# Loading the first quarter of W1 ahead of everything else, and writing the order of the start by hand

## The chip, the core and the metric

The kernel runs on one core of a Trainium2 chip. The metric is the device time of one launch in microseconds. The core's engines work beside each other, each through its own list of instructions in order: TensorE (matrix products), VectorE, ScalarE, GpSimd, and SyncE, which here only issues transfers (DMAs).

## What is computed

Eight batches of 576 rows and 512 columns go through an attention with 32 memory slots per head, a normalised MLP and a gated MLP:

```
a = softmax(phi, over the sequence);  k_m, v_m = a^T k, a^T v      # 8 heads, 32 slots, 64 columns
x = softmax(q k_m^T / 8) v_m                                       # heads side by side: 512 columns
x = x + relu(layernorm(x) * g_ln @ w_ch1) @ w_ch2                  # 512 -> 2048 -> 512
u, v = halves of gelu(x @ w_in)
out = x + (u * (w_sg @ (layernorm(v) * g2) + b_sg)) @ w_out
```

The weights `w_ch1` (W1) and `w_ch2` (W2) come as 64-bit floats, 8.4 MB each.

## The kernel before

`phase1` computes the attention and the first MLP, `phase2` the rest. The first MLP never forms the attention's output for its first product: per batch it multiplies the slot values with the scaled and column-centred W1 (`make_vw`, tiles VW, evicted by `evict_vw` as a high and a low half), and the product `m1` (L592) takes the attention weights aT, high and low, times VW. `relu` splits the result for `m2` (L622 to L624), which multiplies it with the split W2. W1 is used in four quarters of 512 columns, W2 in 16 chunks of 128 rows. For batch 0 the order is: quarter 0 for the first block (256 rows, two tiles of 128) and the second block (320 rows, two tiles of 128 and one of 64), then quarter 1 for both, and so on. `m2` follows three steps behind `m1`.

Ahead of the first `m1` stand the steps of batch 0. `load_phi`, `load_kv`, `load_rem` and `load_q` issue transfers, all through `load` (L85) on SyncE. `prep_max` reduces phi over the sequence on VectorE, transposes on TensorE and lays the maxima on a diagonal (dg); `prep_exp` spreads them, subtracts and takes Exp; `prep_sum` adds on GpSimd and transposes the sums (ptsum); `prep_kv` makes the kv products; `prep_norm` scales them (kvn); `prep_T` transposes (ptk, kvT). `t_q` transposes q, `t_scores` multiplies and starts the softmax on the tile z, `t_norm` and `t_attn` finish it, and `t_attn` writes aT: the high half on ScalarE, the low half on GpSimd for the first two tiles and on VectorE for the others. For W1, `load_w1` brings a quarter in as four raw tiles of 512 KB (two transfers each), `scale_w1` converts them from 64 to 32 bits (`to_f32`: Prelu on ScalarE L112, shift and merge on VectorE L113 and L114) and scales them (ScalarE L498); `center_w1` forms the column means on TensorE (cm, L504) and subtracts them on VectorE (L506, two halves); `store_w1` writes the quarter back for later batches. `split_w2` converts a chunk of W2 with the same steps and splits it.

Every step has a planned time (`at_time`), in units of 1/18 of a batch, and the program is written in the order of these times; negative times lie before the first `m1`. A scheduler that runs when the kernel is built then reorders the instructions of each engine by its own estimate, within their dependencies and within the orders stated by `issue_after`. In the kernel before, gains, phi, k, v and q come first, and the first W1 quarter is loaded at -26.5, scaled at -16.5, the second quarter scaled at -5.0 and centred at -0.3.

## Time and profile before

| | us |
|---|---|
| median of 3 runs | 1208.59 |
| lowest and highest run | 1206.55, 1211.44 |
| span of the profiled execution | 1206.0 |
| first `m1` of batch 0 in it | 49.82 |
| TensorE busy in it | 1167.4 (97%) |

The profile shows one execution. PE is TensorE, PEld its loading of weights, DVE VectorE, ACT ScalarE, POOL GpSimd, SP SyncE; L592 is a line of the kernel. A timeline row has start, duration, engine, line, operation, what it writes and reads, and in brackets the idle time before it with what ended it. In the table of stages each engine has its busy time and, in brackets, its count; the clock is the share of TensorE's full clock that was granted, and a DMA share of 1 is 16 engines full. A busy TensorE counts the whole time of overlapping products, so it is not TensorE at its peak.

### The profile page before, as it was taken

Reading aid. Unit: us, or ns where it says so; the run is one execution under the profiler, and the core shown is the slowest. Engines: PE = TensorE matmul, PEld = TensorE weight load, DVE = VectorE, ACT = ScalarE, POOL = GpSimd, SP = SyncE. Lnnn points to the kernel's source line nnn. Section 1 sums busy time; section 2 is a strip of 40 time slices with the busy share of each in tenths; the row PEclk is TensorE's granted clock in tenths of the full one; section 3 lists DMA queues with packets and bytes.
Section 4 is the critical chain, followed back from the end, with each engine's and each line's share of the span. In section 5 each row is a group of like instructions: output and inputs, shape, how many; then the busy total and the mean of one; then the engine's idle time right before and its main releaser. Section 6 shows DMA issues by size and latency. Waiting matters only on the chain.

```text
span 1206.0 us, 20725 instructions
## 1 busy us (share of the span) xinstructions
PE 1167.4 (97%) x7711; PEld 991.3 (82%) x7711; DVE 689.7 (57%) x1669; ACT 467.1 (39%) x1071; POOL 400.7 (33%) x622
## 2 busy tenths in 40 slices
PE   4699999999999999999999999999999999999998
PEld 2377678888788888788888888889989988998997
DVE  2887665755645545644645445568576477447532
ACT  3575333332432322332323445445444354344430
POOL 2133212211201211201211112456666475566641
PEclk9699999999999999999999999999999999999999
DMA  8996744373341443331410343122240042022201
GB/s 205 284 287 177 219 106 125 79 205 66 109 117 31 129 137 66 97 107 23 128 36 27 106 118 115 35 82 88 77 143 18 19 142 77 1 81 86 79 18 70
DMA packets 199141, 124.15 MB, mean 103 GB/s; under 512 B 93312, under 2 KB 174336, under 8 KB 199040
## 3 DMA queue, kind: packets, MB, share of 16 engines
q1 hardware_dynamic: 199040, 122.82, 36.4%
q8 instruction: 61, 1.00, 0.3%
q14 instruction: 40, 0.33, 0.1%
HBM read 99.72 MB, written 31.33 MB: 109 GB/s over the span
## 4 chain that ended last, share of the span: by engine, by line
PE 86%; DVE 5%; DMA 4%; SPq 2%; issue 1%; POOL 1%; ACT 1%; POOLq 0%; DVEq 0%
PE ph L592 16%; PE py L622 10%; PE py L624 10%; PE py L623 10%; PE pvs L1027 8%; PE po L1050 8%; PE pv L918 8%; PE pu L1002 7%; PE pvw L544 2%; DMA raw<-in_moe_w_ch_dram 2%; SPq L85 2%; PE kvp L315 1%; DMA q<-q_d 1%; PE cm L504 1%; PE sc L401 1%
## 5 line engine op out<-in xcount | busy, mean ns | idle before, releaser
L592 PE MATMUL ph<-aTh,vw 128*128 128x320 f32 (+1 forms) x1024 | 247.2, 300 | 3.5 <-ACT aTh L440 1.4
L622 PE MATMUL py<-whl,hh 128*128 128x512 f32 x512 | 201.8, 396 | 3.0 <-ACT hh L578 3.0
L592 PEld LDWEIGHTS ph<-aTh,vw 128*128 128x128 f32 x1024 | 178.2, 190 | 28.3 <-issue 9.4
L623 PE MATMUL py<-whl,hh 128*128 128x512 f32 x512 | 201.3, 393 | 0.0
L624 PE MATMUL py<-whl,hl 128*128 128x512 f32 x512 | 183.2, 397 | 0.0
L578 ACT ACTIVATE hh<-ph 128x256 fp32r<-128x256 f32 x256 | 96.6, 385 | 167.7 <-PE ph L592 111.5
L579 DVE SCALAR_TENSOR_TENSOR hl<-ph,hh 128x256 fp32r<-128x256 f32 x256 | 106.5, 421 | 87.6 <-ACT hh L578 87.0
L592 PE MATMUL ph<-aTl,vw 128*128 128x256 f32 (+1 forms) x512 | 152.2, 297 | 0.0
L1027 PE MATMUL pvs<-wsh,vhl 128*128 128x288 f32 x576 | 121.0, 295 | 0.0
L622 PEld LDWEIGHTS py<-whl,hh 128*128 128x128 f32 x512 | 96.3, 188 | 26.9 <-ACT hh L578 5.7
L623 PEld LDWEIGHTS py<-whl,hh 128*128 128x128 f32 x512 | 96.5, 189 | 19.3 <-issue 0.8
L1002 PE MATMUL pu<-yTh,whl 128*128 128x288 f32 x512 | 111.0, 296 | 0.3 <-DVE ug L907 0.3
L592 PEld LDWEIGHTS ph<-aTl,vw 128*128 128x128 f32 x512 | 97.1, 190 | 10.3 <-issue 2.9
L624 PEld LDWEIGHTS py<-whl,hl 128*128 128x128 f32 x512 | 89.9, 189 | 12.0 <-issue 2.3
L1027 PEld LDWEIGHTS pvs<-wsh,vhl 128*128 128x128 f32 x576 | 94.4, 188 | 0.6
L918 PE MATMUL pv<-whl,yTh 128*128 128x512 f32 x288 | 91.0, 396 | 0.0
L1050 PE MATMUL po<-whl,gh 128*128 128x512 f32 x288 | 90.0, 391 | 0.0
L1002 PEld LDWEIGHTS pu<-yTh,whl 128*128 128x128 f32 x512 | 85.4, 189 | 1.8 <-DVE ug L907 0.8
L578 ACT ACTIVATE cr<-ph 128x64 fp32r<-128x64 f32 x128 | 28.6, 226 | 130.7 <-PE ph L592 130.1
L1030 POOL TENSOR_TENSOR gt<-gt,ug 128x288 f32<-128x288 f32 x64 | 52.8, 826 | 68.5 <-DVE gt L1029 62.1
L1027 PE MATMUL pvs<-wsl,vhl 128*128 128x288 f32 x256 | 75.6, 295 | 0.0
L1002 PE MATMUL pu<-yTl,whl 128*128 128x288 f32 x256 | 75.5, 295 | 0.0
(154 smaller groups left out, 2162.4 us busy)
## 6 DMA issues: line engine op xcount, KB each, us to landing
wc<-w_d SPq DMA_DIRECT2D x28, 512.0 KB, 6.0
y_d<-x SPq DMA_DIRECT2D x36, 256.0 KB, 2.3
yt<-y_d SPq DMA_DIRECT2D x36, 256.0 KB, 2.7
yr<-y_d SPq DMA_DIRECT2D x36, 256.0 KB, 2.8
kv<-in_k_dram SPq DMA_DIRECT2D x32, 256.0 KB, 3.6
kv<-in_v_dram SPq DMA_DIRECT2D x32, 256.0 KB, 4.0
raw<-in_moe_w_ch_dram SPq DMA_DIRECT2D x32, 256.0 KB, 8.5
raw<-in_moe_w_ch_dram SPq DMA_DIRECT2D x16, 512.0 KB, 6.1
```

What stands on the lines that cost most here:

```text
L85: return nc.sync.dma_start(out=out_ap, in_=in_ap)
L578: high = A.activation(out_h, src, AF.Relu)
L579: return high, V.scalar_tensor_tensor(out=out_l, in0=src, scalar=0.0, in1=out_h.bitcast(F32), op0=ALU.max, op1=ALU.subtract)
L592: R["ph"] = PE.matmul(ph, w_[:, ks], x[:, g, 0:w], start=(n == 0), stop=(n == 3 * HK - 1))
L622: PE.matmul(py, hh, wh, start=start, stop=False)
L623: PE.matmul(py, hh, wl, start=False, stop=False)
L624: PE.matmul(py, hl, wh, start=False, stop=stop)
L918: PE.matmul(pv, y[:, kc, cs], w, start=(n == 0), stop=(n == 3 * KC - 1))
L1002: PE.matmul(pu, w[:, ds_], y[:, kc, cs], start=(n == 0), stop=(n == 3 * KC - 1))
L1027: PE.matmul(pvs, v_, w_, start=(n == 0), stop=(n == len(ops) - 1))
L1030: G.tensor_tensor(out=gt, in0=gt, in1=ug, op=ALU.mult)
L1050: PE.matmul(po, gg[:, dc, cs], w, start=(n == 0), stop=(n == 3 * KC - 1))
```

## The change

The first W1 quarter is loaded first (-60) and converted tile by tile, with its column means formed behind each tile (`mean_w1`), before phi is worked on. Gains, the remainders of phi (prz) and of k and v (kvr), nine transfers in all, are issued by ScalarE while the start is written (`load_small`). All steps up to -0.4 have new times, and every instruction they issue is kept in program order (`keep_in_program_order`, through the class `Traced`, which wraps the engines). `prep_max` is cut in two, the reductions being `prep_red`. Batch 0's softmax of the first two tiles stays ahead of the first `m1`; that of the other three tiles moves behind it (times 0.1 to 1.5), as do three of the four first W2 splits, and the second W1 quarter's scaling (from -5.0 to 1.4) and centring (from -0.3 to 2.4).

```diff
+class Traced:
+    def __getattr__(self, name):
+        f = getattr(self._engine, name)
+        if not self._pinned["on"]:
+            return f
+        return lambda *args, **kw: self._tc.keep_in_program_order(f(*args, **kw))
...
+    def load_small(out_ap, in_ap):
+        return (A if pinned["on"] else SP).dma_start(out=out_ap, in_=in_ap)
...
+        def mean_w1(fb, js):
+            ws = WC[fb]
+            if js[0] == 0:
+                st["cm", fb] = ps_of(fb, [P, DM], "cm")
+            for j in js:
+                PE.matmul(st["cm", fb], mean, ws[j // 2][:, j % 2, :], start=(j == 0), stop=(j == KC - 1))
...
             if b == 0:
+                at_time(-59.9, load_gains)
                 for g in range(2):
+                    at_time(-59.8 + 0.1 * g, load_phi, b, [g])
+                    for part in range(2):
+                        at_time(-59.5 + 0.2 * g + 0.1 * part, load_kv, b, g, part)
+                    at_time(-50 + 0.1 * g, prep_red, b, [g])
+                    at_time(-49.8 + 0.1 * g, prep_max, b, [g])
+                    at_time(-49.4 + 0.1 * g, prep_exp, b, [g])
+                    at_time(-48 + 1.5 * g, prep_kv, b, [g])
+                    at_time(-45, prep_norm, b, g)
+                at_time(-59.45, load_rem, b)
+                at_time(-46, prep_sum, b)
+                at_time(-44.5, prep_T, b)
+                at_time(-40, prep_vb, b)
...
-                        at_time(-27, load_q, us[i], ub, qi)
-                        at_time(-21 + 0.1 * tt, t_q, gr, i)
+                        at_time((-59, -58.5, -58.4)[gi], load_q, us[i], ub, qi)
+                        at_time((-45.5, 0.1, 0.7)[gi], t_q, gr, i)
...
-                    at_time(-17 + 0.1 * tt, t_scores, gr)
-                    at_time(-16 + 0.1 * tt, t_norm, gr)
-                    at_time(-16 + 0.1 * tt, t_attn, gr)
+                    at_time((-43, 0.3, 0.9)[gi], t_scores, gr)
+                    at_time((-42, 0.6, 1.3)[gi], t_norm, gr)
+                    at_time((-41, 0.8, 1.5)[gi], t_attn, gr)
...
+        for j in range(KC):
+            at_time(-51 + 0.1 * j, scale_w1, 0, [j])
+            at_time(-51 + 0.1 * j, mean_w1, 0, [j])
         for fb in range(NFB):
-            at_time((-26.5, -26.2, -2.5, 2.0)[fb], load_w1, fb)
-            at_time((-16.5, -5.0, 3.0, 7.5)[fb], scale_w1, fb)
-            at_time((-16.4, -0.3, 4.6, 9.1)[fb], center_w1, fb)
-            at_time((-15, 1.3, 5.8, 10.3)[fb], make_vw, 0, [fb])
-            at_time((-15, 1.3, 5.8, 10.3)[fb], evict_vw, 0, fb)
-            at_time((1.4, 3.0, 7.4, 12.0)[fb], store_w1, fb)
+            at_time((-60, -58, -2.5, 2.0)[fb], load_w1, fb)
+            if fb:
+                at_time((None, 1.4, 3.0, 7.5)[fb], scale_w1, fb)
+            at_time((-49.5, 2.4, 4.6, 9.1)[fb], center_w1, fb)
+            at_time((-42.8, 2.9, 5.8, 10.3)[fb], make_vw, 0, [fb])
+            at_time((-41.5, 2.9, 5.8, 10.3)[fb], evict_vw, 0, fb)
+            at_time((1.4, 4.0, 7.4, 12.0)[fb], store_w1, fb)
         for c in range(NF):
-            split_at = 4.5 * (c // 4) + 0.5625 * (c % 4) - 0.6 if c > 3 else 0.9 * c - 4
-            at_time(split_at - 5 if c > 3 else -12.7 if c == 3 else 0.2 * c - 26.4, load_w2, c)
+            split_at = 4.5 * (c // 4) + 0.5625 * (c % 4) - 0.6 if c > 3 else (-40.9, 0.4, 1.0, 1.6)[c]
+            at_time(split_at - 5 if c > 3 else 0.02 * c - 58.9, load_w2, c)
             at_time(split_at, split_w2, c)
         ev.sort(key=lambda e: (e[0], e[1]))
+        pinned["on"] = True
         run_until(-0.4)
+        pinned["on"] = False
```

## Rows read from the trace of the kernel before

**Rows 1.** The page: TensorE in 40 slices (tenths busy), chain's end by engine

```profile
PE   4699999999999999999999999999999999999998
...
PE 86%; DVE 5%; DMA 4%; SPq 2%; issue 1%; POOL 1%; ACT 1%; POOLq 0%; DVEq 0%
```

**Rows 2.** Chain of waits of the first 60 us, its shares by line

```profile
by line: DMA raw<-in_moe_w_ch_dram 41.8%; SPq L85 31.4%; DMA kv<-in_v_dram 8.6%; DVE raw L113 3.9%; PE cm L504 3.3%; issue 2.5%; PE ph L592 1.6%; ACT wc L498 1.3%; DVE raw L114 1.0%; DVE aTl L441 1.0%; PE py L624 0.8%; PE px L457 0.4%; PE p
```

**Rows 3.** Stages: length; busy us of PE, PEld, DVE, ACT, POOL; clock; DMA; GB/s

```profile
0.00:26.00 26.00, 13.20 (x142) 8.95 (x142) 6.71 (x17) 7.08 (x15) 7.76 (x22) 1.00 0.80 199
26.00:49.80 23.80, 10.36 (x40) 3.31 (x40) 16.62 (x35) 13.52 (x23) 1.72 (x2) 0.60 1.03 262
49.80:62.57 12.77, 11.57 (x46) 8.31 (x47) 11.89 (x30) 8.18 (x17) 2.59 (x3) 0.80 1.03 331
...
75.89:110.00 34.11, 33.21 (x186) 26.11 (x185) 30.06 (x62) 22.43 (x48) 16.43 (x22) 1.00 0.75 214
110.00:160.00 50.00, 44.87 (x355) 31.71 (x354) 31.16 (x80) 17.22 (x44) 12.25 (x14) 1.00 0.74 197
```

**Rows 4.** Timeline of TensorE, with one row of VectorE: start, us, engine, line

```profile
45.81 3.06 PE L544 MATMUL pvw<-wc,kvT 64*32 64x512 f32 x16 [3.85 <-DVE wc L506]
49.82 0.58 PE L592 MATMUL ph<-aTh,vw 128*128 128x256 f32 x1 [0.95 <-ACT vw L550]
...
51.87 2.43 DVE L113 TENSOR_SCALAR raw<-raw 128x512 uint32<-128x512 uint32 x7
...
57.63 0.28 PE L592 MATMUL ph<-aTh,vw 128*128 128x256 f32 x1
...
62.57 0.31 PE L592 MATMUL ph<-aTh,vw 128*128 128x320 f32 x1
...
75.89 0.28 PE L592 MATMUL ph<-aTh,vw 128*128 128x256 f32 x1
```

**Rows 5.** Timeline of SyncE's queue: start, time taken to issue, transfers

```profile
7.55 0.60 SPq L85 DMA_DIRECT2D kvr<-in_k_dram  x1
...
20.13 36.12 SPq L85 DMA_DIRECT2D raw<-in_moe_w_ch_dram  x32
```

**Rows 6.** Timeline of all engines, the steps of the start

```profile
0.72 1.28 ACT L275 ACT_TABLE_LOAD   x1 [0.72 <-PEq L1109]
...
6.35 1.94 DVE L252 TENSOR_REDUCE pm<-phi 128x128 f32<-128x512 f32 x2 [6.35 <-DMA phi<-in_phi_dram]
...
12.71 0.31 ACT L278 ACTIVATE prz<-prz 64x128 f32<-64x128 f32 x1
...
15.70 0.48 PE L297 MATMUL ptsum<-ident,sm 128*128 128x128 f32 x1 [0.24 <-POOL sm L288]
...
19.29 0.42 DVE L299 TENSOR_REDUCE rs<-ptsum 128x2 f32<-128x256 f32 x1 [6.95 <-PE ptsum L297]
...
22.49 0.64 PE L401 MATMUL sc<-qT,kvT 64*32 64x256 f32 x8
```

**Rows 7.** Groups of instructions of the first 60 us: count, busy us, mean ns

```profile
L112 ACT ACTIVATE raw<-raw 128x512 f32<-128x512 f32 x12 | 8.0, 671 | 10.8 <-DMA raw<-in_moe_w_ch_dram 10.7
L114 DVE SCALAR_TENSOR_TENSOR raw<-raw 128x512 uint32<-128x512 uint32 x12 | 7.9, 682 | 1.1 <-ACT raw L112 1.1
L498 ACT ACTIVATE wc<-raw,g1c 128x512 f32<-128x512 f32 x8 | 6.0, 766 | 3.0 <-DVE raw L114 2.8
...
L506 DVE TENSOR_TENSOR wc<-wc,cm 128x1024 f32<-128x1024 f32 x2 | 2.3, 1214 | 0.0
```

**Rows 8.** Softmax tile z by stages (DVE, ACT, POOL), then timeline rows

```profile
34.00:49.80 15.80, 8.81 (x19) 2.12 (x4) 1.28 (x1) 0.61 1.03 274
...
sum 62.50, DVE 10.55 ACT 3.06 POOL 1.28; mean DVE 3.52 ACT 1.02 POOL 0.43
...
45.77 1.28 POOL L441 TENSOR_TENSOR aTl<-z,aTh 128x512 fp32r<-128x512 f32 x1 [20.91 <-ACT aTh L440]
...
49.80 0.69 DVE L551 TENSOR_TENSOR vw<-pvw,vw 128x512 fp32r<-128x512 f32 x1 [0.69 <-ACT vw L550]
```

More of the change, by code (lines that the diff above doesn't have):

```diff
@@ L30, in fused_kernel @@
     nc = tc.nc
-    PE, V, A, G = nc.tensor, nc.vector, nc.scalar, nc.gpsimd
+    pinned = {"on": False}
+    PE, V, A, G, SP = (Traced(tc, e, pinned) for e in (nc.tensor, nc.vector, nc.scalar, nc.gpsimd, nc.sync))
     B, H, S, D = q.shape
@@ L1088, in phase2 @@
         es_right.close()
-    for g in range(2):
-        load(g1c[64 * g:64 * g + 64, :], g1[g * 4 * D:(g + 1) * 4 * D].rearrange("(c p) -> p c", p=D))
-    load(g2c, g2.rearrange("(c p) -> p c", p=P))
     phase1()
```

85 lines of the change are left out of this document (49 added, 36 removed).

## The prediction, written before the result

> **What bounds the kernel now.** I read the page first. TensorE is busy in nearly every slice but the first, and 86% of the chain that ended last is its own work [rows 1]. So the kernel is a long TensorE stretch behind a start in which TensorE has little to do, and a change to the start is worth what it moves that stretch forward and no more. The second view is the chain of waits of the first 60 us alone: there it is W1 and W2 transfers (41.8%) and SyncE's issuing of transfers (31.4%), not an engine [rows 2]. The third is the table of stages [rows 3]. Up to 26 us the transfers move 199 GB/s, then 262 and 331, with the DMA engines full (share 1.03) from 26 us on. VectorE is busy 16.62 of 23.8 us before the first MLP product and 11.89 of 12.77 us just behind it. From 75.89 to 110 us TensorE is busy 33.21 of 34.11 us, so what reaches that stage earlier ends earlier. The fourth is TensorE's own list [rows 4]: the first MLP product (m1) starts at 49.82, the third m1 of the first block only at 57.63, the first of the second block at 62.57, the first on the second W1 quarter at 75.89.
>
> **What the change does to the transfers.** Before, SyncE issues gains, phi, k, v and q first and reaches W1 at 20.13 us [rows 5]. After, the eight W1 transfers (2.1 MB) lead, then phi and kv (2.8 MB with the remainders), q of the first two tiles (0.5 MB), W2 chunks 0 to 3 (2.1 MB), the rest of q (0.6 MB) and the second W1 quarter. Ahead of the first product 5.4 MB must land. Before, 26.0 us at 199 GB/s moved 5.2 MB although SyncE began with small transfers [rows 3, 5]; so I put the landing of the last needed q near 25 us. W2 and the second half of q then land by about 37 us at 262 GB/s, the second W1 quarter by about 45 us.
>
> **The nine small transfers on ScalarE.** An issue of this kind occupies SyncE for 0.60 us (one of four kvr issues is shown) [rows 5]. No DMA is issued from ScalarE before, so what it costs there is bounded: nothing, or 1.0 us each, of which I take SyncE's 0.60, the nearest row. Nine of them and the table load of 1.28 us [rows 6], from 0.7 us on, leave ScalarE free at 7.4 us, while the first W1 tile should be there at about 5. Queued behind them on ScalarE are W1's conversions and all that follows, so this costs 2.4 us (0 to 6).
>
> The Trainium skill, "DMA: Bandwidth & Descriptors", section "Issuing engines are not separate DMA queues", says that transfers issued by different engines run on the same 16 DMA engines and that a second issuer saves only issue time. That speaks against this part. Before, every transfer of the start leaves SyncE, as these rows of L85 do [rows 5], so no run here shows two issuers. By the rule the part gains SyncE nothing it needs (at 0.60 us per issue it queues 256 KB faster than the data moves), and the sum would be 2.4 us better with the small loads left on SyncE.
>
> **W1 quarter 0.** Its steps are pinned tile by tile on ScalarE: Prelu 0.67, VectorE's merge 0.68, scaling 0.77 [rows 7], some 0.2 for hand-overs: 2.3 us per tile, 9.3 for four, until 16.7 us. VectorE's part ends at 15.8, and only there may the phi maxima start: they stand behind it in the pinned order, though phi has landed. Column means follow each tile on TensorE.
>
> **From phi to the first product.** Before, the phi chain runs from the first maximum at 6.35 to the end of the last Exp at 13.02, 6.7 us [rows 6]; after, the centring (2.35 us in two halves, `center_w1`; the group's mean is 1.21 [rows 7]) is pinned into it, so it takes 9.0: until 24.8. Before, GpSimd's sums begin as that last Exp starts (12.71) and their transpose starts at 15.70, 3.0 us [rows 6]. After, I count these 3.0 from the end of the last Exp, since the pinned order leaves no slack: the transpose starts at 27.8, later than the kv products need if kv lands at 24. From the sums' transpose to the reduction that follows 0.7; from that (19.29) to the scores (22.49) 3.2; the scores 0.64 [rows 6]: 32.3 us. The softmax of the first two tiles: VectorE's work on z is 10.55 us for 1152 columns in three groups [rows 8], so 4.7 for these 512; Exp and hand-overs 0.9; the two evictions of the first W1 product that are pinned into it 1.4 (0.69 each [rows 8]). That is 39.3. Then the high half on ScalarE, 0.7: the first product could start near 40, and flows when GpSimd has the low half, 1.28 later [rows 8]; consecutive VectorE instructions overlap a little (their starts lie closer than their durations), about 0.7 in all. So: first product 39.5, flow from 40.5. Against 49.8 that is **-9.3 us**. Bounds of the flow: with free ScalarE issues 38.1; with 1.0 us per issue, 44.1.
>
> **What is put off.** The softmax of the other tiles and the second quarter's conversion now come behind the first product. VectorE's z work before 49.8 was 8.81 us [rows 8], of which 4.7 belong to the first two tiles; 4.1 us move behind the product, and 1.4 (evictions) move ahead of it. VectorE thus starts the flow 2.7 us poorer, in a stage where it is busy 93% of the time (11.89 of 12.77) [rows 3]: **+2.9 us**. Nothing covers this; if VectorE's waits there shrink it is 0, and if the second block's first product waits for it in the wrong order up to 7. TensorE's granted clock was 0.60 of full before the first product and 0.80 in the stage behind it, that is partly the 1.2 GHz level [rows 3]; after, it idles again before the first product, and I take the same.
>
> **The sum.** 1206.0 - 9.3 + 2.9 = 1199.6 us of span. The median of the runs (1208.59) lies 2.6 above this profile's span; so 1202.2, put at **1202**. By itself this case reaches from 1199 to 1206.
>
> **The rivals.**
> *All of the start is kept* (or more). VectorE's 93% holds work that nothing waited for: the third m1 waited until 57.63 while VectorE worked through seven conversion steps from 51.87 [rows 4]. With a better order the 2.9 vanishes: 1206.0 - 9.3 + 2.6 = 1199.3; with cheap ScalarE issues as well, the flow starts at 38.1, 11.7 earlier: 1196.9. Against it: the work itself is not fewer instructions.
> *Given back in the first quarter.* The second block's first product needs the softmax of three more tiles, whose q lands at about 37 us behind W2. If VectorE takes the second quarter's conversions ahead of it, this product comes at 60 rather than 56 (62.57 less 6.4), and 7 instead of 2.9 are lost: 1206. No difference that shows.
> *The second W1 quarter becomes the bound (slower).* Its conversion moves from ahead of the first product to time 1.4 behind it. If VectorE reaches it only when the second block has its input, at 60 us, the path is four tiles of 2.3, the centring of 2.4, the product of 3.1 as long as it took at the low clock before the first m1 [rows 4], the eviction of 1.4, and some 3 for the last tile's means and the hand-overs: 19. The m1 that stood at 75.89 [rows 4] would stand at 79, 3 later: 1212. It decides once the conversion starts after about 57. For it: the full VectorE. Against: W1 has landed by 45.
> *The change does not do what it says.* If transfers queued behind W1 arrive later than 25 us (all of them share the DMA engines that were full), say q at 35, the chain behind q is unchanged and the first product stays near 49: 1208. Against: 199 GB/s was already reached with small transfers.
>
> **How the numbers follow.** Forecast 0.45, start kept 0.22, given back 0.18, slower 0.11, not done 0.04. A measurement of this kernel can tell about 0.5%, 6 us, from no change: the limit is 1202.5 on the fast side. Of the forecast's own range about two thirds lies beyond it, so faster is 0.30 + 0.22 = 0.52; within 0.15 + 0.18 + 0.04 = 0.37; slower 0.11. The range for 8 in 10 runs from 1195, 1.9 us below the best rival for the spread between runs, to 1210, short of the slow one.
>
> **What would show it.** ScalarE's first Prelu at 7.4 us and one every 2.3 us; the first phi maximum at about 16; the first m1 near 39.5; the first m1 of 320 columns (second block) near 56, and the first on the second quarter near 69.5. A ScalarE issue much shorter or longer than 0.60 moves the first two. If the first m1 comes at 40 and the total moves less than 4 us, the loss is between 40 and 70 us on VectorE; if the total moves by 10, it was not. The prediction is wrong if the loads of the second batch, planned as before, collide in another way: TensorE is busy only 44.87 of 50 us between 110 and 160 [rows 3], and this can turn by 3 us either way.

## The result and the profile after

The changed kernel takes 1217.51 us (median; lowest 1217.13, highest 1218.74) against 1208.37 for the kernel before in the same comparison: a ratio of 1.0076, 95% interval 1.0062 to 1.0091. It is slower by 9 us, and all of the interval lies beyond the 0.5% that the prediction took as the least that can be told. The prediction, 1202 and a range from 1195 to 1210, has the wrong sign. The profiled spans say the same: 1206.0 before, 1215.6 after.

The page, TensorE in 40 slices, to be held against [rows 1]:

```profile
PE   3789989999999999999999999999999999999998
```

Behind the start TensorE fills its slices as before but for one digit (8 for 9, 152 to 182 us). The 9.6 us lie in the first 90. The table of stages, cut at the times of before (columns as in [rows 3]: length, busy us of PE, PEld, DVE, ACT and POOL with counts, clock, DMA share, GB/s):

```profile
0.00:26.00 26.00, 8.24 (x12) 2.38 (x12) 9.79 (x18) 6.63 (x9) 2.88 (x13) 0.97 1.01 258
26.00:49.80 23.80, 14.97 (x167) 9.74 (x168) 10.91 (x23) 11.49 (x23) 4.38 (x6) 0.64 1.02 264
49.80:75.89 26.09, 21.32 (x97) 14.90 (x96) 22.98 (x50) 17.16 (x34) 10.07 (x13) 0.77 0.95 282
75.89:110.00 34.11, 33.95 (x190) 27.06 (x189) 30.84 (x69) 19.79 (x45) 8.64 (x10) 1.00 0.75 214
110.00:160.00 50.00, 44.83 (x333) 34.01 (x331) 29.86 (x76) 19.85 (x49) 15.67 (x18) 0.94 0.54 153
```

The same long stretch behind the first product in the kernel before, which [rows 3] show only in part:

```profile
49.80:75.89 26.09, 24.89 (x130) 19.20 (x131) 23.17 (x54) 18.32 (x38) 4.78 (x4) 0.90 1.04 331
```

VectorE is the row to read. Up to 26 us it does 3.1 us more than before (9.79 against 6.71 [rows 3]): W1's first quarter comes in, and steps of phi move out. From 26 to 49.8 it does 5.7 less (10.91 against 16.62). At 49.8 it is thus 2.6 us behind, and from there it is nearly full in both kernels (22.98 and 23.17 of 26.09), so that it can't catch up. What it has left to do there is another mix, as the softmax tile z shows (columns DVE, ACT, POOL, clock, DMA share, GB/s), for [rows 8]:

```profile
26.00:49.80 23.80, 4.23 (x7) 1.23 (x2) 1.28 (x1) 0.64 1.02 264
49.80:75.89 26.09, 7.63 (x16) 1.86 (x4) 0.00 (x0) 0.77 0.95 282
```

Behind 49.8 VectorE has 7.63 us of softmax, before 1.74 (10.55 less 8.81 [rows 8]). TensorE meanwhile is busy 21.32 us instead of 24.89, at a lower granted clock (0.77, 0.90). From 75.89 on it is as busy as before.

TensorE's timeline after, for [rows 4]: the first m1 and when it flows, the first of its third group of six in the first block (57.63 before), the product for the second W1 quarter, the first m1 of the second block, the first on the second quarter.

```profile
47.70 0.79 PE L630 MATMUL ph<-aTh,vw 128*128 128x256 f32 x2 [0.19 <-ACT aTh L36]
49.12 0.58 PE L630 MATMUL ph<-aTl,vw 128*128 128x256 f32 x1 [0.63 <-POOL aTl L36]
...
52.39 0.58 PE L630 MATMUL ph<-aTh,vw 128*128 128x256 f32 x1
...
72.06 1.92 PE L582 MATMUL pvw<-wc,kvT 64*32 64x512 f32 x16 [3.51 <-DVE pvw L573]
74.08 0.90 PE L630 MATMUL ph<-aTh,vw 128*128 128x320 f32 x2
...
85.89 0.68 PE L630 MATMUL ph<-aTh,vw 128*128 128x256 f32 x1
```

The first m1 comes 2.1 us earlier than before (47.70, 49.82), the second block 11.5 later (74.08, 62.57), the second quarter 10.0 later (85.89, 75.89). Most of this distance stays: the fourth quarter's first m1 comes 9.2 later (138.72, 129.55), and the span is 9.6 longer. TensorE from the first m1 to that of the fourth quarter, before and after (columns as above):

```profile
49.82:129.55 79.73, 77.65 (x476) 59.09 (x477) 62.51 (x139) 46.44 (x98) 25.87 (x29) 0.97 0.83 246
47.70:138.72 91.02, 83.63 (x485) 63.35 (x485) 70.72 (x153) 49.13 (x105) 30.43 (x34) 0.90 0.71 208
```

The length less the busy time is what TensorE waits: 2.1 us before, 7.4 after. Its busy time is 6.0 us longer for nearly the same products (476, 485), at a granted clock of 0.97 before and 0.90 after. Of the 11.3 us by which this stretch is longer, about half is waiting, and the other half is work at a lower clock. This is an account of one profiled execution each; no run shows what the stretch would take at the clock of before.

The start, all engines, for [rows 5] and [rows 6]:

```profile
0.72 1.52 ACTq L36 DMA_DIRECT2D g1c<-in_moe_g_ln_dram  x2
...
3.48 1.79 ACTq L36 DMA_DIRECT2D prz<-in_phi_dram  x2
6.25 0.43 DVE L36 TENSOR_SCALAR raw<-raw 128x512 uint32<-128x512 uint32 x1 [6.25 <-DMA raw<-in_moe_w_ch_dram]
8.11 0.60 ACTq L36 DMA_DIRECT2D kvr<-in_k_dram  x1
...
11.20 1.28 ACT L36 ACT_TABLE_LOAD   x1 [11.20 <-issue]
12.50 0.65 ACT L36 ACTIVATE raw<-raw 128x512 f32<-128x512 f32 x1
...
20.01 1.04 DVE L36 TENSOR_REDUCE pm<-phi 128x128 f32<-128x512 f32 x1
```

ScalarE's nine issues last until 11.2, VectorE shifts the first W1 tile at 6.25, and ScalarE's first Prelu runs at 12.50. The chain of waits of the first 60 us, for [rows 2], shows what holds the issues (its shares by line, then two pieces: start, us, what):

```profile
by line: SPq L36 32.3%; DMA raw<-in_moe_w_ch_dram 21.9%; DMA phi<-in_phi_dram 12.9%; DMA g2c<-in_moe_g_ln_dram 11.3%; DMA kvr<-in_v_dram 8.4%; ACTq L36 2.5%; issue 2.3%; PE ph L630 2.2%; POOL aTl L36 2.1%; ACT raw L127 2.1%; ACT wc L528 1.1
...
2.27 6.75 DMA g2c<-in_moe_g_ln_dram
...
9.04 5.03 DMA kvr<-in_v_dram
```

An issue from ScalarE at 9.04 is released by the landing of g2c, issued at 2.27, and one from SyncE at 14.09 by the landing of kvr, issued at 9.04. The SyncE share stands where it did (32.3%, 31.4% before), W1 and W2 transfers are down from 41.8% to 21.9%, and g2c, kvr and a phi take what they left (the phi of the second batch: this piece begins at 50.47). Then the list of ScalarE with what TensorE and VectorE wait for meanwhile:

```profile
26.86 0.67 ACT L127 ACTIVATE raw<-raw 128x512 f32<-128x512 f32 x1 [5.97 <-DMA raw<-in_moe_w_ch_dram]
...
32.68 0.42 DVE L36 TENSOR_REDUCE rs<-ptsum 128x2 f32<-128x256 f32 x1 [4.41 <-PE ptsum L36]
...
35.83 0.65 ACT L127 ACTIVATE raw<-raw 128x512 f32<-128x512 f32 x1 [5.45 <-DMA raw<-in_moe_w_ch_dram]
...
38.47 0.35 ACT L36 COPY kvT<-ptk 128x256 f32<-128x256 f32 x1
...
38.87 1.11 PE L36 MATMUL sc<-qT,kvT 64*32 64x256 f32 x16 [4.10 <-ACT kvT L36]
...
40.06 0.78 DVE L36 STREAM_TRANSPOSE z<-sc 128x256 f32<-128x256 f32 x2 [5.84 <-PE sc L36]
...
51.91 0.42 DVE L617 SCALAR_TENSOR_TENSOR hl<-ph,hh 128x256 fp32r<-128x256 f32 x1 [2.29 <-ACT hh L616]
```

ScalarE takes Prelus of chunks whose transfers have not landed (5.97 and 5.45 us), the copy kvT stands behind them, the scores behind kvT (4.10), and VectorE behind the scores (5.84). This is where VectorE loses its room: with 4.41 us for the sums' transpose and 2.29 at the end, for the first relu, it stands idle for 12.5 us of this stretch. From 51.91 its own list has no wait worth a row until 74.06, the last piece of the second block's softmax:

```profile
58.30 0.78 DVE L432 STREAM_TRANSPOSE z<-sc 128x256 f32<-128x256 f32 x2
...
60.19 2.96 DVE L129 SCALAR_TENSOR_TENSOR raw<-raw 128x512 uint32<-128x512 uint32 x3
...
68.81 2.34 DVE L544 TENSOR_TENSOR wc<-wc,cm 128x1024 f32<-128x1024 f32 x2
71.07 0.70 DVE L451 STREAM_TRANSPOSE z<-z 128x512 f32<-128x512 f32 x1
...
74.06 0.29 DVE L463 TENSOR_TENSOR aTl<-z,aTh 128x128 fp32r<-128x128 f32 x1 [0.36 <-ACT aTh L462]
74.63 1.29 DVE L589 TENSOR_TENSOR vw<-pvw,vw 128x512 fp32r<-128x512 f32 x2 [0.28 <-ACT vw L588]
```

Softmax steps (L432, L451, L463) and conversion steps (L129, L544) alternate there, so the second block, which needs only the softmax, waits for both. The centring of the second quarter (L544) runs at 68.81; before, it ran at 62.30:

```profile
62.30 2.35 DVE L506 TENSOR_TENSOR wc<-wc,cm 128x1024 f32<-128x1024 f32 x2 [0.88 <-PE cm L504]
```

The second quarter's product is evicted by 75.92 (L589). Its first m1 waits for 10 us more, since in TensorE's list the second block stands ahead of it.

### The profile page after: what moved, and what is told of

It is laid out like the page before. It is cut to its first block, busy times and chain, and to the rows that moved or that the text cites. A ratio compares the mean times of both kernels' runs of the same rounds, so it can differ in the third digit from the quotient of the medians.

```text
span 1215.6 us, 20711 instructions
## 1 busy us (share of the span) xinstructions
PE 1172.8 (96%) x7711; PEld 995.4 (82%) x7711; DVE 692.6 (57%) x1669; ACT 467.2 (38%) x1071; POOL 402.6 (33%) x622
## 4 chain that ended last, share of the span: by engine, by line
PE 84%; DMA 5%; DVE 4%; SPq 2%; issue 1%; ACT 1%; POOL 1%; ACTq 0%; POOLq 0%; DVEq 0%
PE ph L630 15%; PE py L660 10%; PE py L662 10%; PE py L661 10%; PE pvs L1081 8%; PE po L1104 8%; PE pv L972 8%; PE pu L1056 7%; PE pvw L582 2%; SPq L36 2%; PE kvp L337 1%; DMA raw<-in_moe_w_ch_dram 1%; DMA q<-q_d 1%; SPq L97 1%; PE sc L423 1%
## 5 line engine op out<-in xcount | busy, mean ns | idle before, releaser
L630 PE MATMUL ph<-aTh,vw 128*128 128x320 f32 (+1 forms) x1024 | 250.1, 303 | 0.8 <-ACT aTh L462 0.3
```

The source lines that it names most:

```text
L630: R["ph"] = PE.matmul(ph, w_[:, ks], x[:, g, 0:w], start=(n == 0), stop=(n == 3 * HK - 1))
```

## The experiments

All runs in one table. From the profiled execution: the starts of the first m1, of the second block's, of the second quarter's and of the fourth quarter's first m1; what TensorE waits between the first and the last of these (length less busy time); and its granted clock there. Then the median and the ratio to the kernel before.

| kernel | first m1 | block 2 | quarter 2 | quarter 4 | waits | clock | median | ratio, 95% |
|---|---|---|---|---|---|---|---|---|
| before | 49.8 | 62.6 | 75.9 | 129.6 | 2.1 | 0.97 | 1208 | 1 |
| after | 47.7 | 74.1 | 85.9 | 138.7 | 7.4 | 0.90 | 1217.51 | 1.0076 (1.0062 to 1.0091) |
| e1 small loads on SyncE | 46.2 | 73.5 | 85.0 | 136.8 | 7.4 | 0.92 | 1215.02 | 1.0049 (1.0034 to 1.0064) |
| e2 Prelus behind first aTh | 41.9 | 69.5 | 88.3 | 144.6 | 17.9 | 0.91 | 1222.54 | 1.0105 (1.0089 to 1.0122) |
| e3 all softmax ahead | 55.1 | 63.5 | 84.5 | 139.8 | 6.4 | 0.97 | 1219.10 | 1.0083 (1.0068 to 1.0098) |
| e4 softmax, then conversions | 49.1 | 66.4 | 87.0 | 140.4 | 10.5 | 0.94 | 1219.38 | 1.0083 (1.0068 to 1.0098) |
| e5 not pinned | 44.4 | 71.8 | 83.2 | 140.7 | 13.6 | 0.94 | 1220.08 | 1.0093 (1.0070 to 1.0116) |
| e6 = e1 + e2 + e3 | 51.2 | 60.5 | 85.3 | 143.1 | 8.5 | 0.90 | 1222.48 | 1.0114 (1.0096 to 1.0132) |
| e7 first pair, then the rest | 47.0 | 61.3 | 85.3 | 139.5 | 12.7 | 0.94 | 1219.18 | 1.0086 (1.0067 to 1.0104) |
| e8 before, W1 first | 49.3 | 61.7 | 76.9 | 130.7 | 3.0 | 0.95 | 1210.32 | 1.0013 (0.9997 to 1.0029) |
| e9 before, all put off | 46.2 | 70.5 | 90.8 | 142.4 | 11.7 | 0.93 | 1223.29 | 1.0122 (1.0105 to 1.0140) |
| e10 after, nothing put off | 49.5 | 67.4 | 82.9 | 134.1 | 5.0 | 0.93 | 1212.88 | 1.0038 (1.0025 to 1.0051) |
| e11 = e8, Prelus late | 49.5 | 64.9 | 78.4 | 131.4 | 2.4 | 0.93 | 1208.68 | 0.9999 (0.9986 to 1.0011) |
| e12 = e8, ScalarE in order | 42.8 | 58.5 | 72.8 | 130.2 | 6.5 | 0.93 | 1209.64 | 1.0016 (1.0004 to 1.0027) |
| e13 before, softmax put off | 46.7 | 68.4 | 78.3 | 131.0 | 5.0 | 0.96 | 1208.94 | 1.0008 (0.9998 to 1.0018) |
| e14 before, conversions put off | 50.3 | 56.6 | 77.5 | 134.8 | 8.9 | 1.00 | 1214.01 | 1.0054 (1.0036 to 1.0073) |
| e15 = e10, small loads on SyncE | 52.6 | 71.0 | 86.5 | 137.6 | 5.1 | 0.92 | 1215.77 | 1.0066 (1.0049 to 1.0083) |
| e16 = e12, W2 loads earlier | 42.7 | 58.4 | 72.8 | 133.7 | 9.2 | 0.91 | 1212.07 | 1.0030 (1.0014 to 1.0045) |
| e17 before, W2 loads earlier | 48.7 | 62.9 | 76.4 | 131.4 | 5.5 | 0.98 | 1209.46 | 1.0006 (0.9990 to 1.0022) |
| e18 after, conversions not put off | 48.0 | 71.7 | 85.9 | 134.9 | 6.0 | 0.93 | 1214.39 | 1.0047 (1.0031 to 1.0063) |

The first column says nothing about the time: every kernel from 41.9 to 55.1 is there, and the earliest of them is among the slowest. The third nearly orders them: up to 78.4 the time is at most 1210.3 (e14 and e16 are above that), from 82.9 on it is at least 1212.9. The fourth orders them all as far as the medians can be told apart: up to 131.4 the time is at most 1210.3, from 133.7 on it rises with it, from 1212.1. In each of the 19 kernels the profiled span differs from that of before by what this m1 is late, within -1.0 and +1.6 us. So nearly all of each loss is there by then, and little is added behind it.

### Four suspects: ScalarE's issues, its Prelus, the put-off softmax, the pinning

Theory A: the nine issues on ScalarE hold W1 up. Theory B: Prelus that run ahead of their transfers hold ScalarE's list. The others: the softmax of the second block is put off too far; the pinned order is a bad one.

e1, on after:

```diff
-        return (A if pinned["on"] else SP).dma_start(out=out_ap, in_=in_ap)
+        return SP.dma_start(out=out_ap, in_=in_ap)
```

> The nine small transfers of the start go back to SyncE; all else is the changed kernel. Theory A (the issues on ScalarE are what makes the start late): ScalarE has only its table load in front, so the first Prelu comes at the landing of the first W1 tile, near 6.5 us instead of 12.50, and the first m1 near 42 to 43 instead of 47.70. If A were also the cause of the lost total, the time would fall by about 5 us, from 1217.5 to about 1212. Theory C (what is lost is lost behind the first product, where VectorE takes conversions ahead of the softmax of the other three tiles): the first m1 moves as A says, but the first m1 of the second block (320 columns) moves by less than 2 us from 74.08, and the time stays at 1215 to 1218. Rival (the issues cost nothing): first Prelu still near 12, no change anywhere.

The first Prelu moves to 7.14 and the time falls by some 2.5 us, but most of the 5.4 us gained at this Prelu is lost at once. ScalarE's timeline in e1:

```profile
7.14 0.65 ACT L36 ACTIVATE raw<-raw 128x512 f32<-128x512 f32 x1
12.70 0.75 ACT L36 ACTIVATE wc<-raw,g1c 128x512 f32<-128x512 f32 x1 [4.91 <-DMA g1c<-in_moe_g_ln_dram]
```

The scaling behind it waits 4.91 for the gains (g1c), which now stand behind W1 in SyncE's queue.

e2, on after (`first_high` is the high half of aT of the first two tiles):

```diff
-                w = to_f32(raw, [st["hl"]] if fb else None)
+                w = to_f32(raw, [st["hl"]] + [st["first_high"]] * (fb == 1) if fb else None)
...
-            W2[c] = split([raws.pop(("w2", c))], wpool, gate=[gate])
+            W2[c] = split([raws.pop(("w2", c))], wpool, gate=[gate] + [st["first_high"]] * (0 < c < 4))
```

> The Prelus of W2 chunks 1 to 3 and of the second W1 quarter, which the scheduler put between the pinned steps of ScalarE, may come on ScalarE only behind the high half of aT of the first two tiles. Theory B (ScalarE waited in its list for the transfers of these Prelus, 5.97 us at 26.86 and 5.45 us at 35.83): the waits disappear from ScalarE's list, and the first m1 comes near 43 to 44 instead of 47.70. If B were the cause of the lost total, the time would be near 1213. Theory C: the second block's first m1 stays within 2 us of 74.08, and the time between 1215 and 1219.

Theory B is right on the first m1 (41.9) and wrong on the time, which gets worse. Two rows of e2, ScalarE and VectorE:

```profile
42.36 4.00 ACT L127 ACTIVATE raw<-raw 128x512 f32<-128x512 f32 x7
...
48.49 0.42 DVE L619 SCALAR_TENSOR_TENSOR hl<-ph,hh 128x256 fp32r<-128x256 f32 x1 [4.63 <-ACT hh L618]
```

The seven Prelus now stand between the first high half and the first relu; the product waits for that instead, and the second quarter comes at 88.3.

e3, on after (t_q likewise, at -45.5 to -45.3):

```diff
-                    at_time((-43, 0.3, 0.9)[gi], t_scores, gr)
-                    at_time((-42, 0.6, 1.3)[gi], t_norm, gr)
-                    at_time((-41, 0.8, 1.5)[gi], t_attn, gr)
+                    at_time((-43, -42.95, -42.9)[gi], t_scores, gr)
+                    at_time((-42, -41.9, -41.8)[gi], t_norm, gr)
+                    at_time((-41, -40.95, -40.93)[gi], t_attn, gr)
```

> The softmax of all five tiles of batch 0 is pinned ahead of the first product, as it stood before the change; W1 first, the issues on ScalarE and the pinned order stay. Theory C (the other tiles' softmax lost its place to conversions on VectorE): the first m1 comes later, near 53, but the second block's first m1 comes at 58 to 62 instead of 74.08, and the time is 1205 to 1211, no worse than the kernel before. Rival (the second W1 quarter is the bound, and the softmax was only waiting beside it): the first m1 on the second quarter stays at 85 or later, and the time at 1215 or above.

The second block comes at 63.5, 10.6 us earlier than in after, and the time is the same. The second quarter has become late by itself. VectorE's centring and TensorE's first product on that quarter in e3:

```profile
75.77 2.35 DVE L544 TENSOR_TENSOR wc<-wc,cm 128x1024 f32<-128x1024 f32 x2
...
84.53 0.38 PE L630 MATMUL ph<-aTh,vw 128*128 128x256 f32 x1 [1.03 <-ACT vw L588]
```

e4 keeps the softmax behind the first m1 but puts the conversions of quarter 1 and of W2 chunks 2 and 3 behind it on VectorE (planned at 1.55 and 1.52 to 1.6):

```diff
-                w = to_f32(raw, [st["hl"]] if fb else None)
+                w = to_f32(raw, [tiles[4]["tr"] if fb == 1 else st["hl"]] if fb else None)
...
-            gate = st["hl"] if "hl" in st else tiles[1]["tr"]
+            gate = tiles[4]["tr"] if c in (2, 3) else st["hl"] if "hl" in st else tiles[1]["tr"]
```

> Behind the first product, VectorE does the softmax of the other three tiles first; the conversions of the second W1 quarter and of W2 chunks 2 and 3 come behind its last low half. The rest is the changed kernel. Theory C: the first m1 stays at 47.7, the second block's first m1 comes at 58 to 62 instead of 74.08, and the time falls by 7 to 10 us, to 1208 to 1211. Rival (the second W1 quarter is the bound): its first m1 (256 columns, 85.89 before this edit) comes at 86 or later, since its conversion starts later, and the time stays at 1216 or rises.

The second block comes 7.7 us earlier (66.4), the second quarter 1.1 later, the time is again that of after. Softmax and conversions are two locks in a row: opening one leaves the other.

e5, on after:

```diff
-        return lambda *args, **kw: self._tc.keep_in_program_order(f(*args, **kw))
+        return f
```

> The changed kernel with all its new times, the first W1 quarter first and the small transfers on ScalarE, but no instruction of the start is kept in program order. Theory P (the pinned order is what costs): the scheduler fills VectorE's idle time between 28 and 47 us, and the time falls to 1205 to 1210. Theory D (the order within the start matters little; what costs is that conversions and softmax were moved behind the first product, where VectorE has no time left): the first m1 comes somewhere between 42 and 48, but the time stays at 1213 to 1219.

Without the pins the time is 1220.08, no better than after. The pins are not the cause of this loss.

e6 puts e1, e2 and e3 together; e7 takes e1, puts the first pair's softmax first, then the other softmax, and all conversions of quarter 1 and of W2 chunks 1 to 3 behind it (last_exp is the last Exp of batch 0):

```diff
-                w = to_f32(raw, [st["hl"]] if fb else None)
+                w = to_f32(raw, ([tiles[4]["tr"], st["last_exp"]] if fb == 1 else [st["hl"]]) if fb else None)
```

> Three edits together: small transfers on SyncE, the unpinned Prelus behind the first high half on ScalarE, and the softmax of all five tiles pinned ahead of the first product. Theory D: with ScalarE's waits gone, VectorE's softmax starts some 7 us earlier than in the run with the softmax ahead alone; the first m1 comes at 47 to 49 (55.1 there), the second block at 54 to 57, the second quarter (256 columns) at 75 to 79, and the time is 1204 to 1210. Rival Q (the second W1 quarter is the bound wherever the first product stands, as 84.5 to 88.3 in all five kernels so far suggests): second quarter at 84 or later, time 1214 or above.

> Small transfers on SyncE; the first two tiles' softmax first, then the first W2 chunk, then the softmax of the other three tiles, all pinned; the other conversions on ScalarE and VectorE behind that. Theory D: first m1 at 41 to 43, second block at 52 to 55, second quarter at 74 to 79, time 1200 to 1208. Rival Q: the conversions of the second quarter start at about 53 on VectorE instead of 52.25 to 55.42 in the changed kernel, so the second quarter's first m1 stays at 84 or later and the time at 1213 or above.

Both have the second block at 61 and the second quarter at 85.3, and both are slow. Another order of the softmax and fewer waits ahead don't help as long as the conversions come behind.

### Each part alone, on the kernel before

e8, W1 first and nothing else:

```diff
-            at_time((-26.5, -26.2, -2.5, 2.0)[fb], load_w1, fb)
-            at_time((-16.5, -5.0, 3.0, 7.5)[fb], scale_w1, fb)
-            at_time((-16.4, -0.3, 4.6, 9.1)[fb], center_w1, fb)
+            at_time((-60, -26.2, -2.5, 2.0)[fb], load_w1, fb)
+            at_time((-30, -5.0, 3.0, 7.5)[fb], scale_w1, fb)
+            at_time((-29.9, -0.3, 4.6, 9.1)[fb], center_w1, fb)
```

> The kernel before with one part of the change: the first W1 quarter is loaded behind the gains and ahead of phi, and converted and centred there; nothing is pinned, the softmax of all tiles stays ahead of the first product, all transfers stay on SyncE, and the second quarter keeps its times. Theory D: moving the conversion of the first quarter (about 2.3 us per tile) into VectorE's idle time is a gain once nothing else is put off: first m1 at 44 to 48, second quarter at 72 to 76, time 1200 to 1206. Rival L (loading W1 first delays phi, k, v and q by what it gains): first m1 at 49 or later, time 1207 to 1212.

e9, the putting off and nothing else (t_q too, at 0.1 and 0.7; make_vw and evict_vw of quarter 1 at 2.9, its store_w1 at 4.0; the W2 splits behind the softmax of the first two tiles, as in after):

```diff
-                    at_time(-17 + 0.1 * tt, t_scores, gr)
-                    at_time(-16 + 0.1 * tt, t_norm, gr)
-                    at_time(-16 + 0.1 * tt, t_attn, gr)
+                    at_time((-17 + 0.1 * tt, 0.3, 0.9)[gi], t_scores, gr)
+                    at_time((-16 + 0.1 * tt, 0.6, 1.3)[gi], t_norm, gr)
+                    at_time((-16 + 0.1 * tt, 0.8, 1.5)[gi], t_attn, gr)
...
-            at_time((-16.5, -5.0, 3.0, 7.5)[fb], scale_w1, fb)
-            at_time((-16.4, -0.3, 4.6, 9.1)[fb], center_w1, fb)
+            at_time((-16.5, 1.4, 3.0, 7.5)[fb], scale_w1, fb)
+            at_time((-16.4, 2.4, 4.6, 9.1)[fb], center_w1, fb)
...
-            split_at = 4.5 * (c // 4) + 0.5625 * (c % 4) - 0.6 if c > 3 else 0.9 * c - 4
+            split_at = 4.5 * (c // 4) + 0.5625 * (c % 4) - 0.6 if c > 3 else (-4, 0.4, 1.0, 1.6)[c]
```

> The kernel before with the other part of the change alone: the softmax of the third to fifth tile, the scaling and centring of the second W1 quarter and the splits of W2 chunks 1 to 3 get the times behind the first product; the order of the transfers, the queues and the free order of the start stay. Theory D (what was moved behind the first product is what the change pays for): the first m1 comes earlier than 49.82, the second block's first m1 not before 68 and the second quarter's not before 83, and the time is 1213 to 1220, as slow as the changed kernel. If the time stays at 1206 to 1211, the loss is elsewhere: in the pinned order or in the new order of transfers.

This pair decides. W1 first alone changes nothing that can be told (1.0013, 0.9997 to 1.0029). The putting off alone costs 1.22%, 15 us, more than the whole change. Stages of e9, columns as above:

```profile
26.00:49.80 23.80, 16.90 (x73) 7.60 (x74) 13.63 (x24) 14.48 (x26) 2.61 (x2) 0.87 1.03 277
...
75.89:110.00 34.11, 30.38 (x149) 23.01 (x149) 25.01 (x59) 15.53 (x35) 7.17 (x9) 0.90 0.78 223
```

VectorE is busy 13.63 us ahead of 49.8 instead of 16.62 [rows 3], and TensorE 30.38 instead of 33.21 between 75.89 and 110.

Why the early W1 alone brings nothing, TensorE's waits in e8 from 20 to 90 us (total, times, longest):

```profile
PE ph L592 <- ACT aTh L440: 6.3, 1, 6.3
PE sc L401 <- ACT kvT L354: 5.2, 1, 5.2
```

ScalarE is late twice: its list has Prelus of quarter 1 and W2, which wait for transfers, in front of kvT and of aTh. This is theory B on the kernel before.

e13 and e14 take e9 apart. e13 has its softmax lines, with the conversions at their old times; they are now held back only by the softmax of the first two tiles, so that they may take the place that the other softmax leaves. e14 has e9's lines for quarter 1 and its split_at line, with the softmax where it was.

> The kernel before, and of what the change puts off only the softmax of the third to fifth tile (times 0.1 to 1.5); the second quarter and the W2 splits keep their times, behind the first two tiles' softmax. If the softmax is the larger part of the 15 us that both together cost: the second block's first m1 at 68 or later, the time 1215 to 1224. If the conversions are: second block by 66, time 1206 to 1212.

> The kernel before, and of what the change puts off only the second W1 quarter's scaling and centring (1.4, 2.4) and the splits of W2 chunks 1 to 3 (0.4, 1.0, 1.6). If these conversions are the larger part: the second block still at 60 to 64, but the second quarter's first m1 at 82 or later and the time 1214 to 1220. If the softmax is: second quarter at 75 to 78, time 1206 to 1211.

The softmax alone costs nothing that can be told (1.0008), the conversions alone 6.2 us (1.0054). Together they cost 1.22%, twice the 0.62% of the parts' sum. By the table TensorE's waits do add up: against before they are 9.6 us longer in e9, 2.9 in e13 and 6.8 in e14. What does not add up goes with the clock: 0.93 in e9, 0.96 in e13, 1.00 in e14. One execution of each was profiled, and no run tests this.

Neither expectation came in whole. In e13 the second block is late, as the reading with the softmax had it (68.4), and the time is not; e14 has the time of the reading with the conversions, but not its place. Stages of e14:

```profile
75.89:110.00 34.11, 29.42 (x162) 22.27 (x161) 25.47 (x56) 17.60 (x37) 9.57 (x11) 1.00 0.82 243
```

Its second quarter starts at 77.5, where 82 or later was expected, and its TensorE is then busy only 29.42 of 34.11 us: the loss lies behind 75.89, where ScalarE's relu (hh) holds TensorE for 4.0 us in four waits (76 to 136 us).

### Undoing the putting off in the changed kernel

e10 takes after with the softmax of e3 and the conversions at their old times, not pinned from -6 on, and with the Prelus of quarter 1 and of W2 behind the last Exp:

```diff
-                at_time((None, 1.4, 3.0, 7.5)[fb], scale_w1, fb)
-            at_time((-49.5, 2.4, 4.6, 9.1)[fb], center_w1, fb)
+                at_time((None, -5.0, 3.0, 7.5)[fb], scale_w1, fb)
+            at_time((-49.5, -0.3, 4.6, 9.1)[fb], center_w1, fb)
...
-            split_at = 4.5 * (c // 4) + 0.5625 * (c % 4) - 0.6 if c > 3 else (-40.9, 0.4, 1.0, 1.6)[c]
+            split_at = 4.5 * (c // 4) + 0.5625 * (c % 4) - 0.6 if c > 3 else (-4, -3.1, -2.2, -1.3)[c]
...
         pinned["on"] = True
+        run_until(-6)
+        pinned["on"] = False
         run_until(-0.4)
-        pinned["on"] = False
```

> The changed kernel (W1 first, small transfers on ScalarE, start in program order) with what was put off put back: softmax of all five tiles pinned ahead of the first product, second quarter and W2 splits at their times of before and left to the scheduler, their Prelus on ScalarE behind the last Exp of the softmax. Theory D: the first m1 comes at 48 to 50, the second quarter's at 73 to 77, and the time is 1204 to 1210. If the pinned order itself costs, the time stays above 1213.

e18 is after with these lines alone, its softmax still behind the first m1 (quarter 1 is held back by the softmax of the first two tiles only).

> The changed kernel, and only the second W1 quarter (-5.0, -0.3, 1.3) and the W2 splits (-4 to -1.3) have their times of before again, free for the scheduler, behind the softmax of the first two tiles; the other three tiles' softmax stays behind the first product. If the conversions alone account for the loss, as conversions put off alone cost 6.2 us and softmax put off alone 1.1: 1209 to 1212. If both have to be put back together: 1214 to 1218.

e10 gives 1212.88, e18 1214.39: of the 9.1 us, 4.6 come back with everything undone and some 3 with the conversions alone. Both miss what was expected of them if the putting off were all (1204 to 1210, 1209 to 1212). What is left lies in the rest of the change or in e10's own order: it waits 9.1 us for its first aTh, with the whole softmax ahead of it.

e15 is e10 with the edit of e1 and load_gains at -61, ahead of W1, so that the scaling finds its gains.

> The run with what was put off put back (1212.88), and the nine small transfers on SyncE, with the gains ahead of W1 so that the scaling of W1 does not wait for them. Theory A (the issues on ScalarE cost the start): first Prelu at 6 to 8, first m1 2 to 4 us earlier than 49.5, time 1208.5 to 1211. If transfers bound the start in any case, as the run with W1 first alone suggests (49.3 with all on SyncE): first m1 at 48.5 to 50 and time 1212 to 1214, and what is left of the loss then belongs to the pinned order.

The first Prelu comes at 9.54 and scaling follows without the wait of e1. Yet the time is 2.9 us worse than e10's, 1215.77. A row of ScalarE in e15:

```profile
35.17 0.59 ACT L36 COPY qT<-ptq 128x512 f32<-128x512 f32 x1 [4.08 <-PE ptq L36]
```

With the nine issues on it, SyncE issues the first q at 20.74 instead of 18.20 (e10), and the copy of qT waits 4.08 us at 35.17. The Trainium skill, "DMA: Bandwidth & Descriptors", section "Issuing engines are not separate DMA queues", says that a second issuing engine saves only the time of issuing, usually small beside the transfer. The trace agrees for each: one of the nine takes SyncE 0.60 to 0.77 us, and 2.3 to 6.4 us to land. But nine stand in one list, and q behind most of them: with the nine on SyncE the first m1 comes 3.1 us later (52.6 against 49.5). So whether the nine on ScalarE cost or gain depends on what is late: e1 is 2.5 us faster than after, e15 2.9 slower than e10.

### Is there a gain in W1 first?

e11 is e8 with the Prelus of quarter 1 and W2 chunks 0 to 3 behind the last Exp. e12 is e8 with those of quarter 1 and chunk 0 behind the first aTh, and chunks 1 to 3 split behind the first relu (planned at 0.4 to 1.6):

```diff
-            W2[c] = split([raws.pop(("w2", c))], wpool, gate=[gate])
+            W2[c] = split([raws.pop(("w2", c))], wpool, gate=[gate, st["first_high"]] if c == 0 else [*R["relu"]] if c < 4 else [gate])
```

> The run with W1 first alone, and in addition the Prelus of the second W1 quarter and of W2 chunks 0 to 3 on ScalarE come only behind the last Exp of the softmax (there TensorE waited 5.2 us for ScalarE's copy of kvT, behind a Prelu whose transfer had not landed). Theory B: this wait goes, the first m1 comes at 44 to 46 instead of 49.3, the second quarter's at 71 to 74 instead of 76.9, and the time is 1203 to 1207. If those conversions then become the bound, the second quarter stays at 76 or later and the time at 1208 to 1212.

> The run with W1 first alone, and the Prelus of the second W1 quarter and of W2 chunk 0 on ScalarE come behind the first high half of aT; W2 chunks 1 to 3 are split behind the first product's relu, as in the changed kernel. In the run with the gate at the last Exp the first high half stood behind eight Prelus (39.45 to 48.90 us) though its input was there at 40.83. Theory B: the first m1 comes at 42 to 44, the second quarter's at 70 to 74, and the time is 1201 to 1206. Theory D (VectorE's work, not ScalarE's order, is the limit of the stage behind the first product): the first m1 comes at 42 to 44, but the second quarter's not before 76, and the time is 1207 to 1213.

e11 equals the kernel before (0.9999). e12 comes nearest to the start that the prediction had in mind: first m1 at 42.8, 7.0 us earlier than before; second block 4.1, second quarter 3.0 earlier. Still its time is 1209.64 (1.0016, 1.0004 to 1.0027). A stage, then rows of TensorE and ScalarE in e12:

```profile
75.89:110.00 34.11, 30.80 (x170) 23.71 (x170) 26.41 (x59) 19.15 (x41) 13.40 (x20) 1.00 0.75 206
```

```profile
102.52 0.70 ACT L112 ACTIVATE raw<-raw 128x512 f32<-128x512 f32 x1 [1.81 <-DMA raw<-in_moe_w_ch_dram]
...
105.83 0.73 PE L624 MATMUL py<-whl,hh 128*128 128x512 f32 x2 [1.71 <-ACT whl L126]
```

From 75.89 to 110 TensorE is busy 30.80 us, 2.4 less than before [rows 3]. At 105.83 it waits 1.71 for a W2 chunk's high half (whl), and ScalarE had waited 1.81 for the raw chunk at 102.52. So theory E: W2's transfers, issued at times tied to the plan, now come too late. e16 is e12 with them issued earlier, e17 the same on the kernel before as a control:

```diff
-            at_time(split_at - 5 if c > 3 else -12.7 if c == 3 else 0.2 * c - 26.4, load_w2, c)
+            at_time(split_at - 7 if c > 3 else -12.7 if c == 3 else 0.2 * c - 26.4, load_w2, c)
```

> The run with W1 first and its own order on ScalarE (first m1 at 42.84, 7 us earlier than before; third quarter at 96.84, 2.3 earlier; nothing left of it at 108), and W2 chunks 4 to 15 are loaded two planned units earlier, so ahead of most of the transfers of the next batches in SyncE's queue. Theory E (the gain of the start is lost between 97 and 108 us, because the transfers of the third quarter's W2 chunks are queued behind other transfers: ScalarE waited 0.68 and 1.81 us for them, TensorE 1.71 us for the split chunk): these waits go, and the time is 1204 to 1207. Rival (the raw slots or the transfers themselves are the limit there): the waits move elsewhere, time 1208 to 1213.

> The kernel before with the same earlier W2 loads alone, as the control: there TensorE doesn't wait for a W2 chunk between 90 and 110 us, so nothing is to be won, 1206 to 1210; if it is below 1205, the earlier loads are a gain of their own, and what the run beside it gains is theirs.

Theory E fell. e16 is no faster than e12 (1.0030 against 1.0016), and e17 is as before (1.0006). Rows of ScalarE and TensorE in e16:

```profile
95.94 0.67 ACT L112 ACTIVATE raw<-raw 128x512 f32<-128x512 f32 x1 [4.60 <-DMA raw<-in_moe_w_ch_dram]
...
99.74 0.80 PE L624 MATMUL py<-whl,hh 128*128 128x512 f32 x1 [4.71 <-ACT hh L580]
```

The wait has only moved: another Prelu, this time of a W1 tile, waits 4.60 for its transfer, and the relu (hh) behind it on ScalarE holds TensorE for 4.71.

Where e12's lead goes can be read. It is 7.0 us at the first m1, 4.1 at the second block, 3.0 at the second quarter, 2.3 at the third (96.84, 99.12 before) and gone at the fourth (130.21, 129.55). TensorE between the first and the last of these:

```profile
42.84:130.21 87.37, 80.91 (x476) 60.58 (x476) 63.59 (x143) 50.19 (x106) 26.61 (x30) 0.93 0.78 231
```

For the same 476 products as before it waits 4.4 us longer (6.5, 2.1), of which the late W2 chunk is 1.71, and is busy 3.3 us longer (80.91, 77.65), at a granted clock of 0.93 instead of 0.97. So more than half of the lead goes in waits and the rest in work at the lower clock. Which change would keep it is not shown.

## Why the prediction was wrong

- **What bounds the kernel** (a start that ends in a full TensorE stage): right, but "worth what it moves that stretch forward" took the first m1 as the mark of that stretch. By the table it is the fourth quarter's first m1; e2 and e12 move the very first by 7 to 8 us and win nothing.
- **The transfers**: held. TensorE transposes the first q at 32.48 without a wait for it.
- **The ScalarE issues**, 0.60 each and free at 7.4: the duration holds roughly (0.60 to 0.81), but they do not follow each other. After the last of prz, issued by 5.27, the next is kvr at 8.11, and the chain shows a later issue released only by the landing of g2c. The step that failed is nine times 0.60 without the waits of issues for earlier transfers. First Prelu 12.50, not 7.4. The term was 5.1 us too small, and its other end, the issues left on SyncE, was priced as a gain of 2.4: e1 gave that, e15 the opposite.
- **W1 quarter 0**: held; one tile each 2.06 us against 2.3, and the first phi maximum at 20.01, 7.5 us after the first Prelu, in the pinned order as said.
- **From phi to the first product, 39.5**: measured 47.70, and 49.12 in flow. Of the 8.2 us, 4.2 lie ahead of the first phi maximum (20.01, worked out 15.8), 4.0 behind it (27.7 from there to the first m1, worked out 23.7). In e2, where no Prelu of a late transfer stands on this path, it is 23.0 (18.99 to 41.94): the working was sound, but it took the pinned steps to be alone in their lists. The pins hold the steps they cover against each other; Prelus of quarter 1 and W2 (L127, not pinned) still stand between them in ScalarE's list.
- **What is put off, +2.9 (0 to 7)**: the term that decided. VectorE starts the flow "2.7 us poorer": measured 2.6. The step that failed is taking this lag of work for the lag of the path. In a full list that runs in order, what is put off waits for all that stands ahead of it: at a lag of 2.6 us the second block came 11.5 late and the second quarter 10.0. The second quarter's conversion was on VectorE behind the first m1 already before (its centring at 62.30); what changed is that 4.6 us of softmax (8.81 less 4.23) now stand there beside it. Alone, the putting off costs 1.22% (e9). Its larger single part is the conversions (0.54%, e14), which the sum priced at nothing; the softmax, which it did count, costs nothing by itself that can be told (e13). "In the wrong order up to 7" looked for the loss in one order; e3, e4, e6 and e7 are four others and lose as much.
- **The clock** ("I take the same"), a term put at nothing: it did not stay the same. From 49.80 to 75.89 the granted clock is 0.77 after and 0.90 before, and TensorE's work up to the fourth quarter takes 6.0 us longer.
- **The sum**: -9.3 fell to -2.1 at the first m1. From there to the second quarter's first m1 12.1 us were lost (-2.1 to +10.0), to the end of the span 11.7, where the sum has +2.9.
- **The rivals**: "Given back in the first quarter" had the mechanism, conversions ahead of the softmax in VectorE's list, but put the second block at 60 and not at 74.08. "The second W1 quarter becomes the bound" had the sign and the condition (its scaling began at 58.80 on ScalarE, its centring at 68.81). But its path ended at 75.92, ahead of the 79 it worked out; the quarter came at 85.89, since TensorE's list has the second block ahead of it. In e3 and e4, where the second block comes first, the quarter is late by itself. "All of the start is kept" did not come true in e12 either, which has 3.0 of its 7.0 us left at 73 us and none at 130. The evidence against the slow rival, "W1 has landed by 45", told nothing: it was VectorE that came late, with no wait in its list from 51.91 to 74.
- **The check at the end** ("if the first m1 comes at 40 and the total moves less than 4 us, the loss is on VectorE between 40 and 70") nearly fits e12 (42.8, and 1.8 us slower), but there 3 us are lost behind 73, and not on VectorE alone, so that test was too narrow.

Open: how much of the loss is due to the lower clock, since at the full clock TensorE might have waited longer instead; which part of the 4.5 us that e10 still loses is ScalarE's issuing and which the pinned order; and what it would take to keep e12's lead.

## What to carry to other kernels

Before work is put off behind a milestone, look at its engine in the stage that it enters: where that is full (23 of 26 us here), the price isn't the work put off (2.6 us) but the wait of each late result behind all that stands ahead of it (11.5 us). Take as the milestone the point from which nothing more is lost (here the fourth quarter's first product, 80 us behind the very first), not the first product of the bounding engine. Count with the engine's clock, too: here a start with more waits ran at 0.90 of it and not at 0.97. And when an order is written by hand, look at what the scheduler may still move into the same in-order list, above all steps that wait for transfers.

## What the runs showed of the hardware

- A transfer's issue can hold its engine for longer than its own 0.6 us when it waits for an earlier transfer: with 0.60 to 0.81 each, nine issues kept ScalarE until 11.20, with a gap from 5.27 to 8.11, the landing of a transfer issued at 2.27 among what released them.
- A transfer queued behind large ones comes late even if it is small: the gains behind 2.1 MB of W1 held the scaling until 12.70 (4.91 us of waiting) in e1.
- The granted clock differs with the order: from 49.80 to 75.89 us it was 0.90 of full before and 0.77 after, where TensorE was busy 24.89 and 21.32 us. In after TensorE stood idle for the 3.51 us ahead of 72.06. From 72.06 to 75.50 the granted clock was 0.52, which is nearly all the 1.2 GHz level, and 0.99 from there to 85.89; one m1 of 320 columns took 0.47 us at 74.78 and 0.31 at 75.89.
